# A forward transform over D in halves (even and odd columns) in place of quarters (remainders modulo 4), in a fused spectral-filter and GEGLU training step

## The chip, the cores and the metric

The kernel runs on one core of a Trainium2 chip. The core has five engines with a queue each: TensorE (PE in the profile; its weight loads are shown as PEld), VectorE (DVE), ScalarE (ACT), GpSimd (POOL) and SyncE (SP, which here only issues DMAs). The metric is the device time of one execution in microseconds, the median of several runs.

## The reference

Two branches of one layer are mixed by a gate, and the outputs are the layer's value and all gradients of it with respect to the inputs (except `B_x`, which is a constant that the kernel never reads: the FFN branch runs on `A_x`).

```python
x = A_x                                             # (1, 2048, 576), bf16
g = sigmoid((x * gate_w).sum(-1, keepdims=True))
a = irfft2(rfft2(x) * (A_w_r + 1j * A_w_i))         # over S=2048 and D=576; weights (2048, 289)
b = (gelu(x @ B_w_gate) * (x @ B_w_up)) @ B_w_down  # F = 4608
out = g * a + (1 - g) * b
# returned: out, and its vector-Jacobian product with grad_out for
# A_x, A_w_r, A_w_i, B_w_gate, B_w_up, B_w_down, gate_w
```

Both the forward transform of `x` and that of `g * grad_out` are needed: the first for `a` and for the gradient of the spectral weights, the second for the gradient of `x` through the filter and again for that of the weights. All transforms are done as matrix products with tables of sines and cosines.

## The kernel before

**Tiles.** S is split as 16 tiles `t` of 128 rows (row 16 p + t lies on partition p). `xn` and `dB` hold x and grad_out in this form, `xT` and `dOT` hold the transposes: five chunks of columns of D, four of 128 (selected by `eo(c)`) and the last 64 columns, 512 to 575, in the fifth. Because the chunks of `xT` and `dOT` are also the contraction of the FFN's products, the rows of `w_gate`, `w_up` and the transposed `w_down` are loaded in the same order (`load_w`).

**Phase 1** runs over 18 groups `g` of 256 columns of F and in each over four pairs `m` (four tiles of S each; 72 "pairs" in all, numbered `pr`). A pair computes `z` (grad_out times w_down, line 444 and 449) and `xy` (x times w_gate and w_up, line 453 and 460), evacuates them on ACT, forms the derivatives of GELU on DVE, and stores three results to DRAM scratch (`scr`). In the same pair TensorE computes weight gradients of the group before it (`W_units`, line 572, 590, 604). The order on every engine is the program's order, written out by hand; nothing is planned at run time.

**The transforms** ride along in phase 1 as a list `fft` of small units. From pair 6 on, `fft_next` places some four units in each pair between the weight-gradient jobs. First comes the forward transform (`fwd_units`): for each of 16 tiles of x and then of grad_out, `u1` multiplies by the D table (PSUM tile `yps`, evacuated by ACT to `Y`) and `u2` multiplies by the table of the 16-point rotations `R` (PSUM `vps`, evacuated by ACT to `ve`), combines parts on DVE into `Vt`, and stores `Vt` to DRAM. Then come the middle units (filter products) and the inverse. All units and `z` share one PSUM tile of two banks (tag `z`, `bufs=1`), so each must be evacuated before the next.

**The forward transform over D before.** A column d is 4 k + r. `eo(c)` takes every fourth column, so that chunk c of `xT` holds the columns with remainder c. For each remainder, only 73 frequencies need a product (`QF`); the other frequencies are sums and differences of the four remainders' results. `u1` makes four products with 2 x 73 = 146 columns, one for each remainder (line 633), and two with 4 x 73 = 292 columns for the last 64 columns of D (line 636). `u2` makes two products of 292 columns (line 651), and five DVE operations (lines 656 to 663) put the remainders together to 289 frequencies.

**Tables** are built at the start: `iotas` writes index columns on POOL, `build_D` forms angles on DVE or POOL and `sines` evaluates them on ACT. Before, there are three calls: the forward table `D4` (four columns of 73), the tail's `D4` (`D4t`, scaled on POOL by masks of the remainder, line 173), and `Dt` of 145 columns for the inverse, wholly on POOL up to its last step.

**The load of w_down.** For each next group the quarters of the load are issued on SP at the end of the pairs: in pair 0 the parts 0 (w_gate, w_up) and 1 (two transposing DMAs, into `wdT`'s fifth chunk and into `wtmp`), in pair 1 part 2 (a 32 KB copy within `wdT` and the store of `wtmp` to DRAM scratch `wscr`), in pair 2 part 3 (`wscr` back into `wdT` in the order of remainders). The first reader is `z` of the next group, after pair 3.

**Phase 2** (from about 950 us) reads `scr` back and makes the output and the gradient of x, line 1273.

Of the kernel before, what the change touches and what calls it, by code (L numbers as in the profile page):

```python
# [30 lines left out]
FG = 256  # L31
# [10 lines left out]
QF = 73  # L42
# [3 lines left out]
def eo(c):  # L46

    return slice(c, 512, 4)
# [16 lines left out]
def iotas(nc, res, unit):  # L65
    tb = Tables()
    G, V = nc.gpsimd, nc.vector
    kw = dict(allow_small_or_imprecise_dtypes=True)
    tb.halfpi = res.tile([P, 1], F32, name="halfpi")
    V.memset(tb.halfpi[:], math.pi / 2)  # L70
    tb.pi = res.tile([P, 1], F32, name="pi")
    V.memset(tb.pi[:], math.pi * EPS_SCALE)
    tb.warm = res.tile([P, 1], F32, name="warm")
    nc.scalar.activation(tb.warm[:], tb.halfpi[:], ACT.Sin)
    tb.lrow = unit([HF], F32, name="lrow")
    G.iota(tb.lrow[:], pattern=[[1, HF]], base=0, channel_multiplier=0, **kw)
    tb.dcol = res.tile([P, 8], F32, name="dcol")
    G.iota(tb.dcol[:, 0:4], pattern=[[1, 4]], base=0, channel_multiplier=4, **kw)
    for r in (LO, HI):
        G.iota(tb.dcol[r, 4:5], pattern=[[0, 1]], base=512, channel_multiplier=1, **kw)  # L80
    G.iota(tb.dcol[:, 5:7], pattern=[[1, 2]], base=0, channel_multiplier=2, **kw)
    G.iota(tb.dcol[:, 7:8], pattern=[[0, 1]], base=257, channel_multiplier=2, **kw)
    G.iota(tb.dcol[32:64, 7:8], pattern=[[0, 1]], base=256, channel_multiplier=2, **kw)
    tb.dn = res.tile([P, 8], F32, name="dn")
    V.tensor_scalar(tb.dn[:], tb.dcol[:], 1.0 / D, None, op0=ALU.mult)
    tb.late = []
    tb.Dt = []
    tb.Rt = []
    return tb


def iotas_R(nc, tb, res, unit):
# [15 lines left out]
    r4_i = res.tile([P, 1], I32, name="r4_i")  # L108
    tb.r4 = res.tile([P, 5], F32, name="r4_f")

    def parity():
        V.tensor_single_scalar(par_i[:], tb.qcol_i[:], 1, op=ALU.bitwise_and)
        V.tensor_copy(tb.par[:, 1:2], par_i[:])
        V.tensor_scalar(tb.par[:, 0:1], tb.par[:, 1:2], -1.0, 1.0, op0=ALU.mult, op1=ALU.add)
        V.tensor_scalar(tb.kadd[:, 0, 1:2], tb.par[:, 1:2], float(S // 2), float(S // 4), op0=ALU.mult, op1=ALU.add)
        V.tensor_single_scalar(r4_i[:], tb.qcol_i[:], 3, op=ALU.bitwise_and)
        V.tensor_copy(tb.r4[:, 4:5], r4_i[:])
        for r in range(4):
            G.tensor_scalar(tb.r4[:, r:r + 1], tb.r4[:, 4:5], float(r), None, op0=ALU.is_equal)
# [8 lines left out]
def build_D(nc, tb, unit, c0, n, w):  # L128

    V, G = nc.vector, nc.gpsimd  # L130
    step = 2.0 * math.pi / D
    TS = (G if c0 else V).tensor_scalar
    X = unit([n, w], F32, name="XD")
    y = unit([n, w], F32, name="yD")
    for c in range(n):
        TS(y[:, c, :], tb.lrow[:, 0:w], tb.dn[:, c0 + c:c0 + c + 1], MAGIC, op0=ALU.mult, op1=ALU.add)
    TS(y[:], y[:], -MAGIC, -float(D), op0=ALU.add, op1=ALU.mult)
    o = unit([n, 2, w], name="Dt")

    if c0 > 4:  # L140
        for c in range(n):
            G.tensor_scalar(X[:, c, :], tb.lrow[:, 0:w], tb.dcol[:, c0 + c:c0 + c + 1], None, op0=ALU.mult)
        G.tensor_tensor(X[:], X[:], y[:], op=ALU.add)

    def angles():
        for c in range(n if c0 <= 4 else 0):
            V.scalar_tensor_tensor(X[:, c, :], tb.lrow[:, 0:w], tb.dcol[:, c0 + c:c0 + c + 1], y[:, c, :],
                                   op0=ALU.mult, op1=ALU.add)
        V.scalar_tensor_tensor(y[:], X[:], -1.0, X[:], op0=ALU.mult, op1=ALU.max)

    def sines():
        if c0 == 0:
            v = o[:].rearrange("p (o r) c l -> p o (r c) l", o=2)
            co, si = v[:, :, 0:4:3, :], v[:, :, 1:3, :]
            yv, Xv = (t[:].rearrange("p (o r) l -> p o r l", o=2) for t in (y, X))
        else:
            co, si, yv, Xv = o[:, :, 0, :], o[:, :, 1, :], y[:], X[:]
        nc.scalar.activation(co, yv, ACT.Sin, bias=tb.halfpi[:], scale=-step)
        nc.scalar.activation(si, Xv, ACT.Sin, scale=-step * EPS_SCALE)
        if c0 == 0:  # L160
            tb.D4 = o
        elif c0 > 4:
            tb.Dt = [o[:, c] for c in range(n)]

    def tails():
        tl = tb.D4t = unit([2, 2, 4, w], name="Dt")
        G.memset(tl[HI, 0], 0.0)
        G.memset(tl[LO, 1], 0.0)
        for k, h in enumerate((LO, HI)):
            for r in range(4):  # L170
                for c in range(2):
                    b = 3 * c if r % 2 == 0 else 2 - c
                    G.tensor_scalar(tl[h, k, r // 2, b], o[h, 0, c], tb.r4[h, r:r + 1], None, op0=ALU.mult)
    return angles, sines, tails


# [99 lines left out]
def kernel(  # L276
# [24 lines left out]
    wscr = [dram.tile([512, FG], BF16, name=f"wscr{k}") for k in range(2)]  # L301
# [19 lines left out]
    def load_w(g, part, tails=LD):  # L321
# [4 lines left out]
        if part == 0:  # L326
            wgu = wts[g][0]
            for w, c0 in ((B_w_gate, 0), (B_w_up, FG)):
                cols = slice(c0, c0 + FG)
                LD.dma_start(wgu[:, 0:4, cols], w[0:512, fsl].rearrange("(p r) f -> p r f", r=4))  # L330
                for r in (LO, HI):
                    tails.dma_start(wgu[r, 4, cols], w[512:D, fsl])
# [4 lines left out]
        elif part == 2:  # L337
            wdT = wts[g][1]
            LD.dma_start(wdT[LO, 4, :], wdT[HI, 4, :])
            LD.dma_start(wscr[g % 2][:].rearrange("(c p) f -> p c f", p=P), wtmp[0][:])  # L340
        else:
            LD.dma_start(wts[g][1][:, 0:4, :], wscr[g % 2][:].rearrange("(p r) f -> p r f", r=4))
# [282 lines left out]
    def fwd_units(src, dst, scale, ps=pftile):  # L625
        ys = {}

        def u1(t):
            def f():
                yps = ps()  # L630
                for o in range(2):
                    for r, bs in ((2 * o, slice(0, 4, 3)), (2 * o + 1, slice(1, 3))):
                        nc.tensor.matmul(yps[:, o, 0:4 * QF].rearrange("p (b l) -> p b l", b=4)[:, bs, :], lhsT=src[:, r, t, :],  # L633
                                         rhs=tb.D4[:, r], start=(r % 2 == 0), stop=False)
                for o in range(2):
                    nc.tensor.matmul(yps[:, o, 0:4 * QF], lhsT=src[:, 4, t, :],
                                     rhs=tb.D4t[:, t % 2, o].rearrange("p b l -> p (b l)"), start=False, stop=True)
                ys[t] = unit([2, 4 * QF], name="Y")
                if scale is None:
                    nc.scalar.copy(ys[t][:], yps[:, :, 0:4 * QF])  # L640
                else:
                    nc.scalar.activation(ys[t][:], yps[:, :, 0:4 * QF], ACT.Copy, scale=scale[:, t:t + 1])
            return f

        def u2(t):
            def f():
# [3 lines left out]
                for o in range(2):  # L650
                    nc.tensor.matmul(vps[:, o, 0:4 * QF], lhsT=R, rhs=Y[:, o], start=True, stop=True)
                Vt = half([2, DF], name="Vt")
                ve = unit([8, QF], F32, name="ve")
                M = unit([2, 2, 2, QF], F32, name="vm")
                nc.scalar.copy(ve[:].rearrange("p (o b) l -> p o (b l)", o=2), vps[:, :, 0:4 * QF])
                V.tensor_tensor(M[:, 0].rearrange("p u v l -> p v u l"), ve[:, 0:4].rearrange("p (v u) l -> p v u l", u=2),
                                ve[:, 4:8].rearrange("p (v u) l -> p v u l", u=2), op=ALU.add)
                V.tensor_tensor(M[:, 1, 0], ve[:, 0:2], ve[:, 4:6], op=ALU.subtract)
                V.tensor_tensor(M[:, 1, 1], ve[:, 6:2:-3], ve[:, 2:8:5], op=ALU.subtract)
                up = Vt[:, :, 0:2 * (HF - 1)].rearrange("p c (k l) -> p k c l", k=2)[:, :, :, 0:QF]  # L660
                dn = Vt[:, :, DF - 1:0:-1].rearrange("p c (k l) -> p k c l", k=2)[:, :, :, 0:QF - 1]
                V.tensor_tensor(up, M[:, :, :, 0], M[:, :, :, 1], op=ALU.add)
                V.tensor_tensor(dn, M[:, :, :, 0, 0:QF - 1], M[:, :, :, 1, 0:QF - 1], op=ALU.subtract)
# [4 lines left out]
    def tail_table():  # L668
# [4 lines left out]
        for k, r in ((2, P), (3, 32)):  # L673
            o = 512 * (k - 2)
            for c in range(2):
                nc.tensor.transpose(tp_[:, c, o:o + r], tb.Dt[k - 1][0:r, c, 0:P], ident[0:r, 0:r])
            for c in range(2):
                nc.tensor.transpose(tp_[0:n, c, o + 256:o + 256 + r], tb.Dt[k - 1][0:r, c, P:HF], ident[0:r, 0:r])
# [5 lines left out]
        for c in range(2):  # L684
            for e, sb in enumerate((tb.Dt[2][32:64], ot)):
# [263 lines left out]
    D0 = build_D(nc, tb, unit, 0, 4, QF)  # L949
# [4 lines left out]
    D4 = build_D(nc, tb, unit, 4, 1, QF)  # L954
    D2 = build_D(nc, tb, unit, 5, 3, HF)
# [6 lines left out]
    D2[0]()  # L962
# [83 lines left out]
    for g in range(NG):  # L1046
# [3 lines left out]
        for m in range(NPR):  # L1050
# [122 lines left out]
            if m < 3 and g + 1 < NG:  # L1173
                for part in ((0, 1), (2,), (3,))[m]:
                    load_w(g + 1, part)
# [247 lines left out]
```

## Time and profile before

| | |
|---|---|
| median of 3 runs | 1384.02 us (1384.02 to 1384.03) |
| profiled execution | 1384.02 us, span 1382.2 us |
| PE busy | 1363.2 us (99%), 10186 matmuls |
| DVE, ACT, POOL busy | 783.2, 701.6, 259.8 us |
| stretch 0 to 60 us (tables, first group) | PE busy 56.47 |
| stretch 60 to 300 us (forward transform inside it) | PE busy 235.28, DVE 185.10, ACT 180.46 |
| stretch 300 to 950 us (filter and inverse inside it) | PE busy 642.86 |
| stretch 950 to 1382 us (phase 2) | PE busy 428.62 |

Matmuls are pipelined: the profile gives each a duration that reaches to the modelled end of its result, so durations of neighbours overlap, and "busy" is the time in which at least one is under way. What a product costs in a stream is the distance from its start to the start of the next one. In rows of groups, the columns are line, engine, operation, tile written and tiles read, shape, count, then busy time and mean duration, then the idle time of the engine just before and what ended it. A row of the timeline is start, length, engine, line, operation and count; rows of one operation that follow each other are merged.

### The profile page before, as it was taken

Reading aid. Unit: us, or ns where it says so; the run is one execution under the profiler, and the core shown is the slowest. Engines: PE = TensorE matmul, PEld = TensorE weight load, DVE = VectorE, ACT = ScalarE, POOL = GpSimd, SP = SyncE. Lnnn points to the kernel's source line nnn. Section 1 sums busy time; section 2 is a strip of 40 time slices with the busy share of each in tenths; the row PEclk is TensorE's granted clock in tenths of the full one; section 3 lists DMA queues with packets and bytes.
Section 4 is the critical chain, followed back from the end, with each engine's and each line's share of the span. In section 5 each row is a group of like instructions: output and inputs, shape, how many; then the busy total and the mean of one; then the engine's idle time right before and its main releaser. Section 6 shows DMA issues by size and latency. Waiting matters only on the chain.

```text
span 1382.2 us, 25988 instructions
## 1 busy us (share of the span) xinstructions
PE 1363.2 (99%) x10186; PEld 908.5 (66%) x10272; DVE 783.2 (57%) x1514; ACT 701.6 (51%) x1300; POOL 259.8 (19%) x513
## 2 busy tenths in 40 slices
PE   9999999999999999999999999999999999999998
PEld 6556656566556556556656566556777777777776
DVE  7887777865988877885676766550001642122101
ACT  7877777768877877866766767651000000000000
POOL 7001110132445444331110111110000110000000
PEclk9999999999999999999999999999999999999999
DMA  7434444466466665555556556659999997787773
GB/s 234 126 88 136 128 131 119 120 169 158 129 162 159 161 160 150 143 156 151 135 157 154 159 158 166 168 128 274 196 190 197 235 193 164 158 161 168 155 150 88
DMA packets 512423, 218.95 MB, mean 158 GB/s; under 512 B 312010, under 2 KB 503180, under 8 KB 512300
## 3 DMA queue, kind: packets, MB, share of 16 engines
q1 hardware_dynamic: 495178, 191.89, 59.3%
q0 software_dynamic: 14912, 24.24, 6.1%
q8 instruction: 80, 1.31, 0.4%
q10 hardware_dynamic: 2210, 1.15, 0.4%
q14 instruction: 43, 0.35, 0.1%
HBM read 45.51 MB, written 98.30 MB: 104 GB/s over the span
## 4 chain that ended last, share of the span: by engine, by line
PE 92%; ACT 3%; DVE 2%; DMA 1%; issue 1%; ACTq 0%; SPq 0%; DVEq 0%
PE acc L1273 31%; PE wps L590 16%; PE xy L460 16%; PE wps L572 10%; PE z L444 8%; PE wps L604 2%; PE xy L453 2%; PE z L449 2%; DMA wgu<-in_B_w_up_dram 1%; DMA xn<-in_A_x_dram 1%; PE pf L914 1%; PE pf L840 1%; PE pf L751 1%; PE pf L633 1%; PE pf L916 1%
## 5 line engine op out<-in xcount | busy, mean ns | idle before, releaser
L1273 PEld LDWEIGHTS <-pin 128*128 128x128 bf16 x3456 | 337.5, 98 | 86.3 <-issue 0.3
L590 PE MATMUL wps<-dH,xn 128*128 128x512 bf16 x1135 | 270.0, 379 | 0.9
L460 PE MATMUL xy<-wgu,xT 128*128 128x512 bf16 x1083 | 258.6, 380 | 8.2 <-issue 6.8
L460 PEld LDWEIGHTS <-xT 128*128 128x128 bf16 x1152 | 106.4, 98 | 132.9 <-issue 24.8
L590 PEld LDWEIGHTS <-xn 128*128 128x128 bf16 x1152 | 111.4, 98 | 118.4 <-issue 0.6
L1290 ACT COPY bo<-acc 128x288 f32<-128x288 f32 x32 | 12.8, 399 | 305.0 <-PE acc L1273 271.6
L572 PE MATMUL wps<-dB,A 128*128 128x288 bf16 x1152 | 153.3, 286 | 0.1
L597 POOL DMA_DIRECT2D out_dram<-dw x134 | 72.8, 547 | 421.9 <-ACT dw L541 380.4
L1273 PE MATMUL acc<-wgT,pin 128*128 128x288 bf16 x1152 | 143.8, 286 | 0.0
L1273 PE MATMUL acc<-wuT,pin 128*128 128x288 bf16 x1152 | 143.6, 286 | 0.0
L1273 PE MATMUL acc<-wd_all,pin 128*128 128x288 bf16 x1152 | 142.6, 286 | 0.0
L444 PE MATMUL z<-wdT,dOT 128*128 128x256 bf16 x1152 | 137.7, 273 | 0.0
L572 PEld LDWEIGHTS <-A 128*128 128x128 bf16 x1152 | 112.0, 98 | 33.0 <-issue 0.3
L472 ACT ACTIVATE da<-z,omg 128x256 bf16<-128x256 f32 x288 | 112.0, 471 | 31.9 <-PE z L449 31.8
L444 PEld LDWEIGHTS <-dOT 128*128 128x128 bf16 x1152 | 112.3, 98 | 21.6 <-issue 0.6
L1345 DVE SCALAR_TENSOR_TENSOR f32t<-gwf,dlog,b16t 128x576 f32<-128x576 f32 x16 | 13.1, 818 | 171.8 <-DMA b16t<-dxa_scr 171.8
L481 ACT CAST xb<-xy 128x512 bf16<-128x512 f32 x144 | 85.0, 590 | 48.2 <-PE xy L460 48.2
L479 ACT ACTIVATE q<-xy 128x512 bf16<-128x512 f32 x144 | 87.8, 613 | 17.0 <-PE xy L460 13.5
L482 ACT CAST hu<-xy 128x512 bf16<-128x512 f32 x144 | 87.4, 607 | 0.0
L518 DVE TENSOR_TENSOR xb<-xb,sg 128x1024 bf16<-128x1024 bf16 x48 | 33.1, 690 | 85.8 <-ACT sg L510 85.7
L541 ACT CAST dw<-wps 128x512 bf16<-128x512 f32 x72 | 42.3, 590 | 54.8 <-PE wps L590 52.4
L1304 DVE SCALAR_TENSOR_TENSOR b16t<-b16t,g,f32t 128x576 bf16<-128x576 bf16 x16 | 13.1, 818 | 98.1 <-DMA b16t<-a_scr 97.9
(239 smaller groups left out, 1700.3 us busy)
## 6 DMA issues: line engine op xcount, KB each, us to landing
scr<-dH SPq DMA_DIRECT2D x144, 256.0 KB, 3.4
scr<-A SPq DMA_DIRECT2D x72, 256.0 KB, 2.5
out_dram<-dw POOLq DMA_DIRECT2D x134, 64.0 KB, 2.5
wd_all<-in_B_w_down_dram SPq DMA_DIRECT2D x3, 1728.0 KB
out_dram<-dwd POOLq DMA_DIRECT2D x34, 144.0 KB, 2.9
scr_p<-Vt SPq DMA_DIRECT2D x32, 145.0 KB, 2.8
wgu<-in_B_w_gate_dram SPq DMA_DIRECT2D x18, 256.0 KB, 4.1
wgu<-in_B_w_up_dram SPq DMA_DIRECT2D x18, 256.0 KB, 3.4
```

Of the source, the lines that this page charges most:

```text
L444: nc.tensor.matmul(zo(t), lhsT=dOT[:, ci, t, :], rhs=wdT[:, ci, :], start=(t % 4 < 2 and ci == 0), stop=False)
L460: nc.tensor.matmul(xy[k][:, t % 2, :], lhsT=xT[:, ci, t, :], rhs=wgu[:, ci, :], start=False, stop=(ci == 3))
L472: nc.scalar.activation(da[:, t, :], z[:, t % 2, t // 2, :], ACT.Copy, scale=omg32[:, 4 * m + t:4 * m + t + 1])
L479: nc.scalar.activation(q[:, h, :], xy[:, :, 0:FG], ACT.Square)
L481: nc.scalar.copy(xb[:, h, :], xy[:, :, 0:FG])
L482: nc.scalar.copy(hu[:, h, :], xy[:, :, FG:2 * FG])
L518: V.tensor_tensor(xb[:], xb[:], s[:], op=ALU.mult)
L541: wcopy[0](out, in_)
L572: nc.tensor.matmul(wps[:, :288], lhsT=tl(0, t)[:, fch * P:(fch + 1) * P], rhs=dB[:, t, h * 288:(h + 1) * 288], start=(t == 0), stop=(t == ...
L590: nc.tensor.matmul(wps[:].rearrange("p a b -> p (a b)"), lhsT=xn[:, t, c * P:(c + 1) * P], rhs=kt[t // 4][1][:, t % 4].rearrange("p k f -> ...
L597: wst[0].dma_start(ov[:, c, fsl], dw[:, k, :])
L1273: nc.tensor.matmul(acc[:, :288], lhsT=src[:, r, :], rhs=w_of(r)[:, h * 288:(h + 1) * 288], start=(first and r == 0), stop=(last and r == F ...
```

## The change

The forward transform goes over the two parities of d instead of the four remainders. `eo(c)` now takes 128 columns of one parity (c = 0, 1 the even ones, 2, 3 the odd ones, below 512). The table of the forward transform is that of 145 columns (`HF`) for each chunk, the same that the inverse uses, so the separate quarter table is gone. `u1` makes four products of 290 columns and two of 290 for the tail; `u2` two of 290, and two DVE operations in place of five. The tail's table is scaled on DVE by the two parity masks instead of on POOL by four remainder masks. `build_D` is called for two, two and one columns of 145. In `load_w`, `wdT` gets its rows from `wtmp` by four copies within SBUF, without the DRAM scratch, and the parts 0, 1 and 2 are issued at the ends of pairs 0, 1 and 2. The rows of w_gate and w_up are loaded in the new order by as many DMAs as before.

```diff
 def eo(c):
-    return slice(c, 512, 4)
+    return slice(256 * (c % 2) + c // 2, 256 * (c % 2) + 256, 2)
...
-    G.iota(tb.dcol[:, 0:4], pattern=[[1, 4]], base=0, channel_multiplier=4, **kw)
+    for par in range(2):
+        G.iota(tb.dcol[:, 2 * par:2 * par + 2], pattern=[[256, 2]], base=par, channel_multiplier=2, **kw)
...
-        for r in range(4):
-            G.tensor_scalar(tb.r4[:, r:r + 1], tb.r4[:, 4:5], float(r), None, op0=ALU.is_equal)
...
     def tails():
-        for k, h in enumerate((LO, HI)):
-            for r in range(4):
-                for c in range(2):
-                    b = 3 * c if r % 2 == 0 else 2 - c
-                    G.tensor_scalar(tl[h, k, r // 2, b], o[h, 0, c], tb.r4[h, r:r + 1], None, op0=ALU.mult)
+        for k, r in enumerate((LO, HI)):
+            for par in range(2):
+                V.tensor_scalar(tl[r, k, par], o[r, 0], tb.par[r, par:par + 1], None, op0=ALU.mult)
...
     def load_w(g, part, tails=LD):
-                LD.dma_start(wgu[:, 0:4, cols], w[0:512, fsl].rearrange("(p r) f -> p r f", r=4))
+                LD.dma_start(wgu[:, 0:4, cols].rearrange("p (e k) f -> p e k f", e=2),
+                             w[0:512, fsl].rearrange("(k p e) f -> p e k f", e=2, p=P))
...
-        elif part == 2:
+        else:
             wdT = wts[g][1]
             LD.dma_start(wdT[LO, 4, :], wdT[HI, 4, :])
-            LD.dma_start(wscr[g % 2][:].rearrange("(c p) f -> p c f", p=P), wtmp[0][:])
-        else:
-            LD.dma_start(wts[g][1][:, 0:4, :], wscr[g % 2][:].rearrange("(p r) f -> p r f", r=4))
+            for par in range(2):
+                for h, r in enumerate((LO, HI)):
+                    LD.dma_start(wdT[r, 2 * par:2 * par + 2, :], wtmp[0][par:P:2, h:4:2, :])
...
         def u1(t):
-                for o in range(2):
-                    for r, bs in ((2 * o, slice(0, 4, 3)), (2 * o + 1, slice(1, 3))):
-                        nc.tensor.matmul(yps[:, o, 0:4 * QF].rearrange("p (b l) -> p b l", b=4)[:, bs, :], lhsT=src[:, r, t, :],
-                                         rhs=tb.D4[:, r], start=(r % 2 == 0), stop=False)
-                for o in range(2):
-                    nc.tensor.matmul(yps[:, o, 0:4 * QF], lhsT=src[:, 4, t, :],
-                                     rhs=tb.D4t[:, t % 2, o].rearrange("p b l -> p (b l)"), start=False, stop=True)
+                for par, j in [(par, j) for par in range(2) for j in range(2)] + [(0, 2), (1, 2)]:
+                    ci, tab = (4, 4 + 2 * (t % 2) + par) if j == 2 else (2 * par + j, 2 * par + j)
+                    nc.tensor.matmul(yps[:, par, :2 * HF], lhsT=src[:, ci, t, :], rhs=tb.Dt[tab].rearrange("p c l -> p (c l)"),
+                                     start=(j == 0), stop=(j == 2))
...
         def u2(t):
-                M = unit([2, 2, 2, QF], F32, name="vm")
-                V.tensor_tensor(M[:, 0]..., ve[:, 0:4]..., ve[:, 4:8]..., op=ALU.add)
-                V.tensor_tensor(M[:, 1, 0], ve[:, 0:2], ve[:, 4:6], op=ALU.subtract)
-                V.tensor_tensor(M[:, 1, 1], ve[:, 6:2:-3], ve[:, 2:8:5], op=ALU.subtract)
-                V.tensor_tensor(up, M[:, :, :, 0], M[:, :, :, 1], op=ALU.add)
-                V.tensor_tensor(dn, M[:, :, :, 0, 0:QF - 1], M[:, :, :, 1, 0:QF - 1], op=ALU.subtract)
+                V.tensor_tensor(Vt[:, :, 0:HF], v[0], v[1], op=ALU.add)
+                V.tensor_tensor(Vt[:, :, DF - 1:HF - 1:-1], v[0][:, :, 0:HF - 1], v[1][:, :, 0:HF - 1], op=ALU.subtract)
...
-    D0 = build_D(nc, tb, unit, 0, 4, QF)
+    D0 = build_D(nc, tb, unit, 0, 2)
     D0[0]()
...
-    D4 = build_D(nc, tb, unit, 4, 1, QF)
-    D2 = build_D(nc, tb, unit, 5, 3, HF)
+    D2 = build_D(nc, tb, unit, 2, 2)
+    D2[0]()
+    D4 = build_D(nc, tb, unit, 4, 1)
...
-    D2[0]()
...
             if m < 3 and g + 1 < NG:
-                for part in ((0, 1), (2,), (3,))[m]:
-                    load_w(g + 1, part)
+                load_w(g + 1, m)
```

## The prediction

> **What bounds the kernel now.** I read the page first: the busy shares and the chain that ended last.
>
> ```profile
> PE 1363.2 (99%) x10186; PEld 908.5 (66%) x10272; DVE 783.2 (57%) x1514; ACT 701.6 (51%) x1300; POOL 259.8 (19%) x513
> PE 92%; ACT 3%; DVE 2%; DMA 1%; issue 1%; ACTq 0%; SPq 0%; DVEq 0%
> ```
>
> TensorE (PE) is busy for 99% of the span and is 92% of the chain; 1382.2 less 1363.2 leaves 19.0 us in which it stood idle anywhere. But a share is a mean over stages, and the change sits in one of them, the forward transform. Line 633, the first product of the transform, runs from 75 to 280 us by the view of that line, so next comes the table by stretches around it. Columns: length, then busy time of PE, its weight loads, DVE, ACT and POOL, the granted TensorE clock, and the DMA share.
>
> ```profile
> 60.00:100.00 40.00, 37.64 (x271) 23.11 (x274) 33.91 (x72) 32.75 (x63) 5.69 (x10) 1.00 0.43 119
> 100.00:150.00 50.00, 49.35 (x362) 30.82 (x365) 38.90 (x83) 36.68 (x67) 6.47 (x12) 1.00 0.44 124
> 150.00:200.00 50.00, 49.53 (x352) 30.30 (x356) 38.38 (x80) 37.02 (x70) 5.40 (x10) 1.00 0.46 130
> 200.00:250.00 50.00, 49.42 (x359) 30.58 (x363) 37.91 (x80) 36.45 (x66) 5.39 (x10) 1.00 0.45 126
> 250.00:300.00 50.00, 49.34 (x359) 30.55 (x363) 36.00 (x76) 37.55 (x69) 8.57 (x16) 1.00 0.46 130
> ```
>
> PE idles 2.36 + 0.65 + 0.47 + 0.58 + 0.66 = 4.7 us of these 240. DVE is busy for 185.1 of the 240 (77%): well loaded, but it has 55 us to spare, and the clock is at full rate throughout. Whom PE waits for here is in the view of waits of PE over 60 to 300 us (total, times, longest):
>
> ```profile
> PE xy L460 <- issue: 1.6, 10, 0.2
> PE pf L651 <- ACT Y L640: 1.1, 1, 1.1
> PE pf L633 <- ACT ve L655: 1.0, 2, 0.7
> ```
>
> No wait of PE on DVE is there at all. The two that name an engine are on ACT. So in this stage matmul columns are what time is made of.
>
> **The products of u1 (line 633 and 636), by the timeline of PE:**
>
> ```profile
> 207.28 0.41 PE L651 MATMUL pf<-Y,Rt 128*128 128x292 bf16 x2
> 207.54 1.02 PE L460 MATMUL xy<-wgu,xT 128*128 128x512 bf16 x4
> 208.40 1.89 PE L590 MATMUL wps<-dH,xn 128*128 128x512 bf16 x8
> 210.13 0.43 PE L633 MATMUL pf<-Dt,dOT 128*128 128x146 bf16 x4
> 210.39 0.41 PE L636 MATMUL pf<-Dt,dOT 128*128 128x292 bf16 x2
> 210.64 1.02 PE L590 MATMUL wps<-dH,xn 128*128 128x512 bf16 x4
> ...
> 212.75 1.15 PE L572 MATMUL wps<-dB,A 128*128 128x288 bf16 x8
> ```
>
> Only starts are used, since the ends are modelled and overlap. Today u1 is four products of 146 columns in 210.39 - 210.13 = 0.26 us (65 ns each) and two of 292 in 210.64 - 210.39 = 0.25 us: 0.51 us. The changed u1 is six products of 290 columns with the same six stationary tiles. The nearest row is L572: eight products of 288 columns from 212.75 to 213.73, where the next group starts, so 122.5 ns each. With two columns more I take 124 ns: 6 x 124 = 0.74 us. The difference is 0.23 us, and u1 runs 32 times (16 tiles of x, 16 of grad_out): **+7.3 us on PE**. Bounds: at 122 ns a product it is 0.22 x 32 = +7.0; at the 130 ns that a pair of L651 takes (207.28 to 207.54) it is (0.78 - 0.51) x 32 = +8.6. Nothing hides it, because PE has nothing else to stand behind.
>
> The Trainium skill, "TensorE: Matmul & The Clock Gate", section "Back-to-back issue gap", sets the gap at N/2.4 + 2.5 ns, and says besides that a stream in which every matmul loads its own weights holds about 81 ns at N=128. By that second figure four narrow products would cost at least 0.32 us today, u1 0.57 us, and the change only about +5.4 us (estimate from that page). The row above has 65 ns each with a weight load apiece, so here the row decides.
>
> **u2, PE side.** Two products of 292 columns become two of 290; at 0.42 ns a column, (379 - 286)/(512 - 288) by the mean durations of L590 and L572, that is 128 columns in all, 0.05 us. Nothing.
>
> **u2, DVE side.** Today's five operations, from the groups by form (busy, mean ns, idle before):
>
> ```profile
> L656 DVE TENSOR_TENSOR vm<-ve 128x292 f32<-128x292 f32 x32 | 14.7, 461 | 20.0 <-ACT ve L655 19.6
> L658 DVE TENSOR_TENSOR vm<-ve 128x146 f32<-128x146 f32 x32 | 9.7, 304 | 0.0
> L659 DVE TENSOR_TENSOR vm<-ve 128x146 f32<-128x146 f32 x32 | 9.7, 303 | 0.0
> L662 DVE TENSOR_TENSOR Vt<-vm 128x292 bf16<-128x292 f32 x32 | 14.8, 464 | 1.1
> L663 DVE TENSOR_TENSOR Vt<-vm 128x288 bf16<-128x288 f32 x32 | 14.7, 459 | 1.1
> ```
>
> They sum to 1.99 us. The changed u2 has two, of 290 and 288 columns; the same shape (the inverse's yo, line 925 and 926) takes 493 and 479 ns, so 0.97 us. DVE loses 1.02 x 32 = 33 us of work between 75 and 293 us. On the path this is worth what PE waits for DVE there, which is 0 by the waits. The bound on the gain is every named engine wait of PE in the stretch, 1.1 + 1.0, and 0.2 for the turn of R: -2.3 us. I take 0, for the releasers are ACT, and ACT's copies hardly shrink (584 to 580 columns). The unit of scratch that u2 no longer takes frees ring space; PE waits for none of it.
>
> **The load of wdT (load_w).** The third quarter of each group no longer writes wtmp to DRAM and reads it back, it copies it within SBUF: one DMA of 32 KB as before, and four of 64 KB. Per group SP issues 6 at the end of pair 0, 2 transposes at the end of pair 1 and 5 at the end of pair 2, against 8, 2 and 1 today. What has to be met is the first z of the next group. Group 5 is the tightest I found:
>
> ```profile
> 248.73 0.68 SPq L342 DMA_DIRECT2D wdT<-wscr  x1
> ...
> 256.95 1.26 PE L444 MATMUL z<-wdT,dOT 128*128 128x256 bf16 x10
> ```
>
> 8.2 us lie between issue and use (9.0 for the group at 411 us, 9.3 at 720 us). Five issues at 0.68 us put the last at 248.73 + 2.7 = 251.4. A copy inside SBUF of today lands by this row:
>
> ```profile
> wdT<-wdT SPq DMA_DIRECT2D x17, 32.0 KB, 3.3
> ```
>
> 251.4 + 3.3 = 254.7, so 2.2 us ahead of z: cost 0. Behind the five on SP stands the store of Vt, issued at 255.45 today when DVE has written it; SP is free from 249.4, so the queue is clear again at 252.1. The transposes move one pair later, to the end of pair 1 (230.16 here), land in 3.7 us by the median of wtmp in the view of DMAs and are first read 15 us later. If each copy held SP as long as a transpose does (1.3 us), the last would be issued at 248.73 + 0.68 + 3 x 1.3 = 253.3 and, landing in 5.8 us as the loads of Vp from scr_g do by the same view, arrive at 259.1: 2.2 us late here, 1.4 and 1.1 at the two next. So 0 to +4.7 us; I take 0, by the nearest row, which is the copy to the same tile.
>
> The Trainium skill, "DMA: Bandwidth & Descriptors", section "Anatomy of one DMA — SWDGE (gpsimd) path", gives about 2.0 us fixed per DMA (for another path than SP's), which speaks against splitting. If that were paid one after another, four copies would add 8 us and z of group 5 would wait (estimate). But the six wgu loads of a group issue within 3.9 us and land together here, so the fixed part overlaps.
>
> **Start.** Tables are wider (145 columns for 73), but fewer, and 16 scalings on POOL (9.9 us from 13.93) become four on DVE. DVE begins its tables when dn is there, at 2.7 us, and reaches the copy of the w_down tile at 5.94. Changed: two products with the column (0.25 each), one scaling (0.45), two STT (0.4), one of 290 (0.56) for the first half, and 0.4 x 2 + 0.56 for the second, which now stands ahead of that copy: about 6.3, so the copies come up to 0.4 us later; two index fills fewer (0.15 each) take that back. The tail table's four on DVE, at most 0.36 each by the 128x576 scaling of dB, start at 11.6 and end by 13.0, under the 1.28 us that DVE waits there until 13.12; were that cover gone, 1.4 us. First used at 75 us. I take 0. The gain is bounded by the waits of PE for DVE before 60 us, 0.8 for a copy of dOT and 0.3 at the gate: -1.1; the loss by the 0.4 above.
>
> **Sum.** Profiled execution: 1384.02 us, span 1382.2, so 1.8 us outside it; the median of the three runs is the same 1384.02. +7.3 + 0 + 0 + 0 + 0 gives **1391.3 us**.
>
> **Rivals.**
> 1. *The added columns fall partly into standing waits.* The 2.3 us of ACT waits lie where ACT is late (the sines of R near 80 to 91 us); longer u1 gives ACT time. With the bound of the start, +7.3 - 2.3 - 1.1 = +3.9: 1387.9. Against it: waits elsewhere in the stretch are nearly nil. Chance 0.12.
> 2. *wdT becomes the wait.* z stands first in each group, so all of PE stands. Price +4.7 from the three tightest: 1396; if SP also is blocked behind a store at the end of pair 2 in most of 17 groups, 1 us each, +17: 1408. It begins when issue to landing exceeds 8.2 us. For it: SP is often held for DVE (107 us for Vt in total). Against it: the estimate of 6.0 us. Chance 0.09.
> 3. *Not slower: DVE paced the stage after all.* The relief of 33 us would reach PE through u2: ve and Vt freed sooner, and the one PSUM tile that z and the units share handed over sooner. It decides from 0.23 us of hidden PE wait per tile and would, at a third of the relief, give -11 + 7.3: 1380. Against it: eight L590 fill 208.40 to 210.13 at 216 ns each, the rate of the four L460 before them (207.54 to 208.40), so no gap is hidden where L633 takes over. Chance 0.06.
>
> **How the numbers follow.** My forecast (wide products at their rate, nothing else moves) gets 0.73, from +6 to +8.6. The range reaches below to rival 1 and above into the smaller part of rival 2: 1387.9 to 1395.0. About 0.2% (2.8 us) is what a measurement can tell from no change. Slower by more: forecast, rivals 1 and 2, less what rival 1 may exceed: 0.93. Within: 0.04, faster 0.03, both of rival 3.
>
> **What would show it.** Right: u1 six products in 0.74 us; PE idle of 60 to 300 us again near 5 us while DVE's busy time there falls by some 33 us; z of group g+1 waiting for no wdT copy; the time before phase 2 longer by 7 us and phase 2 (line 1273) unchanged. Wrong: a pitch of 290 columns below 115 ns; a wait of L444 for a DMA into wdT; the first z after 8.5 us; PE idle in the stage falling by more than 2.5 us.

## The result and the profile after

The changed kernel takes 1389.87 us (median of 6 runs, 1389.5 to 1390.37) against 1384.03 us before in the same session. The ratio is 1.0039, with a 95% interval from 1.0026 to 1.0052, so the change costs 5.8 us. The forecast was 1391.3 us in a range from 1387.9 to 1395.0, slower.

The page of the changed kernel, the busy shares and the chain that ended last:

```profile
PE 1370.5 (99%) x10186; PEld 913.3 (66%) x10272; DVE 752.4 (54%) x1418; ACT 702.8 (51%) x1300; POOL 245.4 (18%) x486
PE 95%; ACT 2%; DVE 2%; issue 1%; POOL 0%; ACTq 0%; DVEq 0%; POOLq 0%
```

It has as many matmuls as before, 7.3 us more of busy TensorE, 30.8 us less of busy DVE, and a longer span. The stretches around the forward transform (columns as before: length, then PE, its weight loads, DVE, ACT, POOL, clock, DMA share, GB/s):

```profile
100.00:150.00 50.00, 49.36 (x346) 30.81 (x348) 28.89 (x55) 35.20 (x65) 5.79 (x11) 1.00 0.39 113
200.00:250.00 50.00, 49.58 (x345) 30.74 (x348) 28.44 (x53) 35.75 (x63) 6.46 (x12) 1.00 0.40 109
```

DVE has fallen from 38.90 and 37.91 to 28.89 and 28.44 us of each 50. TensorE is as full as it was, and it gets through fewer matmuls in the same time (346 and 345 against 362 and 359), because those of u1 are wider. The timeline of PE shows one u1:

```profile
211.60 1.89 PE L570 MATMUL wps<-dH,xn 128*128 128x512 bf16 x8
213.33 0.91 PE L613 MATMUL pf<-Dt,dOT 128*128 128x290 bf16 x6
214.08 1.02 PE L570 MATMUL wps<-dH,xn 128*128 128x512 bf16 x4
```

Six products of 290 columns fill 213.33 to 214.08, 0.75 us, where four of 146 and two of 292 took 0.51.

To see where the 5.65 us between the two spans (1387.9 and 1382.2, by the trace 1387.89 and 1382.24) arose, I take the same five events in both traces: the first product of z in group 0, in group 1, in pair 6 (where the transforms begin to be placed), in pair 23 (the forward transform is done) and in the last pair. The rows of the kernel before come first, then those of the changed one:

```profile
7.73 0.38 PE L444 MATMUL z<-wdT,dOT 128*128 128x256 bf16 x2
43.80 0.27 PE L444 MATMUL z<-wdT,dOT 128*128 128x256 bf16 x1
67.38 0.38 PE L444 MATMUL z<-wdT,dOT 128*128 128x256 bf16 x2
298.92 0.38 PE L444 MATMUL z<-wdT,dOT 128*128 128x256 bf16 x2
915.68 0.38 PE L444 MATMUL z<-wdT,dOT 128*128 128x256 bf16 x2
```

```profile
7.53 0.39 PE L424 MATMUL z<-wdT,dOT 128*128 128x256 bf16 x2
42.67 0.38 PE L424 MATMUL z<-wdT,dOT 128*128 128x256 bf16 x2
66.20 0.38 PE L424 MATMUL z<-wdT,dOT 128*128 128x256 bf16 x2
304.74 0.38 PE L424 MATMUL z<-wdT,dOT 128*128 128x256 bf16 x2
921.44 0.38 PE L424 MATMUL z<-wdT,dOT 128*128 128x256 bf16 x2
```

| stretch | before, us | after, us | difference |
|---|---|---|---|
| to the first z | 7.73 | 7.53 | -0.20 |
| to group 1 | 36.07 | 35.14 | -0.93 |
| to pair 6 | 23.58 | 23.53 | -0.05 |
| forward transform | 231.54 | 238.54 | **+7.00** |
| filter and inverse | 616.76 | 616.70 | -0.06 |
| to the end | 466.56 | 466.45 | -0.11 |

So the forward transform costs 7.0 us more, within 0.3 us of the forecast's 7.3, and the first 44 us give 1.1 us back, which the forecast had set to nothing. The row to the first z says little: in the twelve traces of this case, of both kernels and of the experiments, that instant lies anywhere between 7.32 and 8.43 us. The row to group 1 repeats: the changed kernel and the four experiments on it that do not hold up its start have 35.01 to 35.14 us there.

Most of the gain to group 1 is seen at one place, 0.67 of the 0.93 us. The timelines of DVE and of POOL before, then of both after:

```profile
29.09 1.12 DVE L523 TENSOR_SCALAR xb<-s 128x1024 bf16<-128x1024 bf16 x1
29.05 0.87 POOL L243 IOTA k2B<- 128x128 f32 x1
```

```profile
28.66 0.43 DVE L503 TENSOR_SCALAR xb<-s 128x1024 bf16<-128x1024 bf16 x1
25.04 0.88 POOL L223 IOTA k2B<- 128x128 f32 x1
```

The same scaling of 128x1024 took 1.12 us before, beside an index fill of POOL (IOTA) that began 0.04 us earlier. It took 0.43 us after, when POOL had begun that fill at 25.04. DVE was that much later with its copy of dOT, and TensorE waited for this copy 0.8 us before and 0.2 us after, by the waits of PE over the first 60 us, before and after:

```profile
PE pf L399 <- DVE dOT L406: 0.8, 1, 0.8
```

```profile
PE pf L379 <- DVE dOT L386: 0.2, 1, 0.2
```

The other 0.25 us lie at the gate's products: from the first of them to the next z it takes 1.01 us before, with a wait of 0.28 for DVE, and 0.76 us after, without. DVE had begun its last copies of xT there at 9.82 before and at 9.41 after. What brought them forward was not tested on its own.

POOL came to its fills earlier. Before, the 16 scalings of the tail table stood ahead of them and kept POOL until 23.85 us. After, they are gone and POOL's other tables are done sooner, so that it stands idle for 12.80 us and goes on at 20.58, when DVE's values are there. That was read from the traces; the second set of experiments asks whether the fill beside the scaling is the cause.

### The profile page after: what moved, and what is told of

Same layout as the page of the kernel before. It is cut to its first block, busy times and chain, and to the rows that moved or that the text cites. A ratio compares the mean times of both kernels' runs of the same rounds, so it can differ in the third digit from the quotient of the medians.

```text
span 1387.9 us, 25926 instructions
## 1 busy us (share of the span) xinstructions
PE 1370.5 (99%) x10186; PEld 913.3 (66%) x10272; DVE 752.4 (54%) x1418; ACT 702.8 (51%) x1300; POOL 245.4 (18%) x486
## 4 chain that ended last, share of the span: by engine, by line
PE 95%; ACT 2%; DVE 2%; issue 1%; POOL 0%; ACTq 0%; DVEq 0%; POOLq 0%
PE acc L1245 31%; PE xy L440 17%; PE wps L570 17%; PE wps L552 10%; PE z L424 9%; PE wps L584 2%; PE xy L433 2%; PE pf L613 2%; PE z L429 2%; PE pf L887 1%; PE pf L813 1%; PE pf L630 1%; PE pf L724 1%; PE pf L889 1%; PE pf L860 1%
```

## The experiments

The theory: the forward transform pays for its columns on TensorE, DVE's relief and the new load of wdT are worth nothing, and the start gains about 1 us. The rivals: DVE paces the stage in part, or the load of wdT carries part of the result.

**A dose of narrow products, in the kernel before.**

```diff
                 yps = ps()
+                for r in range(4):
+                    nc.tensor.matmul(yps[:, r // 2, 292:438].rearrange("p (b l) -> p b l", b=2), lhsT=src[:, r, t, :],
+                                     rhs=tb.D4[:, r], start=True, stop=True)
                 for o in range(2):
```

> The kernel before, with four more products of 146 columns in each u1, into columns 292 to 437 of the same PSUM tile that nothing reads; the results stay as they were. Theory (TensorE columns set the time of the forward transform): four at 65 ns, 32 times, +8.4 us, so 1392.4. Rival (DVE paces the stage and TensorE has room): no change, 1384.0 within 1 us.

Measured: 1391.89 us against 1384.2 in the same session, ratio 1.0047 (1.0034 to 1.0059): +7.7. One u1 in its timeline of PE:

```profile
215.11 0.42 PE L632 MATMUL pf<-Dt,dOT 128*128 128x146 bf16 x4
215.38 0.42 PE L636 MATMUL pf<-Dt,dOT 128*128 128x146 bf16 x4
215.64 0.41 PE L639 MATMUL pf<-Dt,dOT 128*128 128x292 bf16 x2
```

The added four take 0.27 us (215.11 to 215.38) and come through almost whole: TensorE has no room in this stage, and the rival, that DVE paces it and TensorE has room, falls.

**DVE's work put back, in the changed kernel.**

```diff
                 v = [ve[:, 0], ve[:, 1]]
+                M = unit([8, 73], F32, name="vm")
+                vf = ve[:].rearrange("p o c l -> p (o c l)")
+                Mf = M[:].rearrange("p b l -> p (b l)")
+                V.tensor_tensor(Mf[:, 0:292], vf[:, 0:292], vf[:, 288:580], op=ALU.add)
+                V.tensor_tensor(Mf[:, 292:438], vf[:, 0:146], vf[:, 290:436], op=ALU.subtract)
+                V.tensor_tensor(Mf[:, 438:584], vf[:, 146:292], vf[:, 434:580], op=ALU.subtract)
```

> The changed kernel, with three DVE operations added to each u2 that take the 292, 146 and 146 columns of the kernel before into a tile that nothing reads: 32 times 1.07 us, 34 us of DVE work. Theory: TensorE does not wait for DVE there, so 1389.9 within 0.5 us. Rival (the relief of DVE paid for the part by which the measured +5.8 us stays under the +7.3 us of the columns): 1391.3 or more.

Measured: 1389.85 us, against 1389.87 for the changed kernel without it. The view of waits of PE over 60 to 300 us of this run:

```profile
PE pf L613 <- ACT ve L633: 1.0, 2, 0.7
PE pf L630 <- ACT Y L618: 0.8, 1, 0.8
```

These are the changed kernel's own two waits, with 25.0 us more of busy DVE in that stretch (176.38 against 151.37; neighbours overlap, so this is less than the 34 us of their durations). By the starts of z the forward transform takes 238.53 us, against 238.54 without this work. So three quarters of the 33.7 us of which the change relieved DVE here (185.10 to 151.37) were worth nothing; that the last quarter was worth nothing too is argued from the waits, for in neither kernel does TensorE wait for DVE in this stretch.

**The DRAM trip of wdT put back, in the changed kernel.**

```diff
-        else:
+        elif part == 2:
             wdT = wts[g][1]
             LD.dma_start(wdT[LO, 4, :], wdT[HI, 4, :])
-            for par in range(2):
-                for h, r in enumerate((LO, HI)):
-                    LD.dma_start(wdT[r, 2 * par:2 * par + 2, :], wtmp[0][par:P:2, h:4:2, :])
+            LD.dma_start(wscr[g % 2][:].rearrange("(c p) f -> p c f", p=P), wtmp[0][:])
+        else:
+            LD.dma_start(wts[g][1][:, 0:4, :].rearrange("p (e k) f -> p e k f", e=2),
+                         wscr[g % 2][:].rearrange("(k p e) f -> p e k f", e=2, p=P))
...
-                load_w(g + 1, m)
+                for part in ((0, 1), (2,), (3,))[m]:
+                    load_w(g + 1, part)
```

> The changed kernel, with the load of wdT as before: wtmp to DRAM and back, in the four parts of the old order. Theory: hidden in both forms, 1389.9 within 0.5 us. Rival (the shorter path without DRAM traffic is what gave 1.5 us back): 1391.3. Second rival (the five copies at the end of pair 2 are late for z): 1389 or less.

Measured: 1389.66 us, against 1389.87 without the trip. The interval of the ratio (1.0023 to 1.0046) shuts out the first rival's 1391.3 but not the second's 1389. The traces shut out that too: from group 1 to the last pair every stretch agrees with the changed kernel's within 0.02 us, and neither run's waits of PE, over the whole span, name a load of wdT. Both forms of the load are hidden.

**Half of the main products left out, in the changed kernel.**

```diff
-                for par, j in [(par, j) for par in range(2) for j in range(2)] + [(0, 2), (1, 2)]:
+                for par, j in [(0, 2), (1, 2)] + [(par, j) for par in range(2) for j in range(2)]:
                     ci, tab = (4, 4 + 2 * (t % 2) + par) if j == 2 else (2 * par + j, 2 * par + j)
-                    nc.tensor.matmul(yps[:, par, :2 * HF], lhsT=src[:, ci, t, :], rhs=tb.Dt[tab].rearrange("p c l -> p (c l)"),
-                                     start=(j == 0), stop=(j == 2))
+                    n = 2 * HF if j == 2 else 146
+                    nc.tensor.matmul(yps[:, par, :n], lhsT=src[:, ci, t, :], rhs=tb.Dt[tab].rearrange("p c l -> p (c l)")[:, 0:n],
+                                     start=(j == 2), stop=(j == 1))
```

> The changed kernel, with the four main products of u1 cut to their first 146 columns (the other half of the transform is left out, so the output is not the reference's; the tail's two products stay whole and come first). Theory: the whole loss is the columns, 4 x (126 - 66) ns x 32 = 7.7 us less, 1382.2, which is below the kernel before because the start got faster by 1.2 us. Rival (part of the loss is elsewhere in the change): 1384 or more.

Measured: 1382.51 us against 1384.2 before, ratio 0.9983 (0.9974 to 0.9992), and 7.4 us under the changed kernel. With the columns of u1 back at about the width of before (four of 146 and two of 290), all of the loss is gone, the forward transform takes 231.10 us against 231.54 before, and the kernel is below its predecessor by 1.7 us. In its timeline of PE the six products run from 213.04 to 213.54, 0.50 us:

```profile
213.04 0.67 PE L614 MATMUL pf<-Dt,dOT 128*128 128x290 bf16 x6
213.54 0.65 PE L552 MATMUL wps<-dB,A 128*128 128x288 bf16 x4
```

**The start: two orders of the tail table, in the kernel before.** The first issues the 16 scalings behind the index fills; the second has DVE scale the table.

```diff
         parity()
-        D4[2]()
...
                 elif m == 1:
                     next(makeB)
+                    D4[2]()
```

> The kernel before, with the 16 scalings of the tail table on POOL issued after the index fills of the table B (in pair 1 instead of pair 0). Theory (the start of the changed kernel is faster because POOL's index fills no longer run beside a DVE scaling at 29 us, which took 1.12 us in place of 0.43): that DVE operation is short again, TensorE's wait of 0.83 us at 34.84 goes, 1383.0 to 1383.4. Rival (the start gained from fewer and differently ordered table operations on DVE): 1384.0.

```diff
             for r in range(4):
-                for c in range(2):
-                    b = 3 * c if r % 2 == 0 else 2 - c
-                    G.tensor_scalar(tl[h, k, r // 2, b], o[h, 0, c], tb.r4[h, r:r + 1], None, op0=ALU.mult)
+                bs = slice(0, 4, 3) if r % 2 == 0 else slice(2, 0, -1)
+                V.tensor_scalar(tl[h, k, r // 2, bs], o[h, 0], tb.r4[h, r:r + 1], None, op0=ALU.mult)
```

> The kernel before, with the tail table scaled on DVE in 8 operations of 146 columns instead of 16 on POOL. Theory: as the last one, -0.8 us from the wait at 34.84, less up to 0.7 us if the 8 operations (2 us) outlast DVE's pause of 1.28 us at 12 us: 1383.2 to 1383.9. Rival: 1384.0 or more.

Measured: 1384.57 us (1383.11 to 1386.24) and 1383.77 us (1383.72 to 1384.79), against 1384.31 in the same session; ratios 0.9996 (0.9987 to 1.0005) and 0.9993 (0.9984 to 1.0002). The times can't tell either from no change, and the first missed its forecast of 1383.0 to 1383.4. The trace of the first can tell the mechanism. In its timelines of DVE and POOL the fill of k2B is at 25.80 and the DVE scaling is short again; in its waits of PE the wait is down to 0.2 us.

```profile
29.44 0.43 DVE L523 TENSOR_SCALAR xb<-s 128x1024 bf16<-128x1024 bf16 x1
25.80 0.87 POOL L243 IOTA k2B<- 128x128 f32 x1
```

```profile
PE pf L399 <- DVE dOT L406: 0.2, 1, 0.2
```

From the first z (8.13) to that of group 1 (43.52) it takes 35.39 us, against 36.07 before: 0.68 us of the changed kernel's 0.93 by the order on POOL alone. In the second the eight DVE operations outlast DVE's pause and cost more than was allowed for: the same stretch takes 36.56 us. Its time lies in the forecast range all the same, which is luck as far as the trace tells: its profiled execution is 0.3 us shorter than that of the kernel before because it gains 0.5 us from the last pair on, where nothing was changed.

**Sixteen scalings put back on POOL, in the changed kernel**, into a tile that nothing reads.

```diff
+        idle = unit([16, 73], name="idle")
+        for k, r in enumerate((LO, HI)):
+            for b in range(8):
+                nc.gpsimd.tensor_scalar(idle[r, 8 * k + b], o[r, 0, 0, 0:73], tb.par[r, 0:1], None, op0=ALU.mult)
```

> The changed kernel, with 16 scalings of 64x73 on POOL (9.9 us in the kernel before) put back after the tail table, into a tile that nothing reads, so that POOL reaches the index fills as late as before. Theory: a DVE scaling is stretched by one of the fills again and TensorE waits 0.7 to 0.8 us more, 1390.6 to 1390.8. Rival: 1389.9.

Measured: 1389.93 us, no change where 1390.6 to 1390.8 was expected. It could not test whether a fill holds up a scaling: the scalings ran from 11.16 for 9.09 us, POOL was done at 20.25 and began its next work at 20.44, when DVE's values were there, and the fill of k2B came at 24.89 (25.04 without them). It shows that the 16 scalings alone do not make POOL late. In the kernel before they do, because there POOL begins them 2.8 us later, at 13.93, and ends at 23.85. The next two experiments put work right ahead of the fills.

**Eight more index fills, and eleven scalings instead, in the changed kernel.**

```diff
+    spin = unit([2, 2, 16, 2], F32, name="spin")
+    for _ in range(8):
+        G.iota(spin[:], pattern=[[0, 4], [2, 16], [0, 2]], base=0, channel_multiplier=0, **kw)
     G.iota(k2[:], pattern=[[0, 4], [2, 16], [0, 2]], base=0, channel_multiplier=0, **kw)
```

> The changed kernel, with eight more index fills of 128x128 on POOL (0.87 us each, 7 us) ahead of those of the table B, into a tile that nothing reads; they run from about 25 to 32 us. The run with 16 scalings put back did not test the theory, because POOL was done with them before it could begin the fills. Theory (an index fill on POOL holds up a DVE scaling that runs beside it): two to three of the DVE scalings between 28 and 33 us take 0.8 to 1.2 us in place of 0.43, TensorE's wait at 33.7 grows from 0.16 by 0.8 to 1.9 us, 1390.7 to 1391.8. Rival (the long DVE scaling before was chance, or came from something else): all stay at 0.43, 1389.9.

```diff
+    spin = unit([3, HF], F32, name="spin")
+    G.memset(spin[:], 0.0)
+    for _ in range(11):
+        G.tensor_scalar(spin[:], spin[:], 0.5, 1.0, op0=ALU.mult, op1=ALU.add)
     G.iota(k2[:], pattern=[[0, 4], [2, 16], [0, 2]], base=0, channel_multiplier=0, **kw)
```

> As the last, with eleven scalings of 128x435 fp32 on POOL (some 7 us by the 626 ns of such a one before) in place of the eight index fills. Theory (it is the index fill that holds DVE): DVE's scalings stay at 0.43 and the time at 1389.9. Rival (any work on POOL does it): as the run with the fills, 1390.7 to 1391.8.

Measured: 1390.81 us with the fills (ratio to before 1.0043, 1.0029 to 1.0057), +0.9 over the changed kernel; 1394.01 us with the scalings (1.0066, 1.0051 to 1.0082), +4.1. The first interval covers the changed kernel's 1.0039, so there the trace has to decide: to group 1 it takes 36.30 us, against 35.14 without the fills. The timelines of DVE and POOL and the waits of PE of the run with the fills:

```profile
31.32 0.62 DVE L470 TENSOR_SCALAR s<-q 128x1024 bf16<-128x1024 bf16 x1
32.65 1.04 DVE L472 TENSOR_SCALAR q<-q 128x1024 bf16<-128x1024 bf16 x1
32.54 0.86 POOL L226 IOTA k2B<- 128x128 f32 x1
```

```profile
PE pf L382 <- DVE dOT L389: 1.0, 1, 1.0
```

Two of DVE's three scalings in that stretch take 0.62 and 1.04 us in place of 0.42, its operations on two tensors keep their 0.69, and TensorE's wait is back, at 1.0 us. So an index fill can hold up a DVE scaling, and that wait is on the path. It does not always: the third scaling ran among the fills too and took its 0.43 us. Its row and those of two fills:

```profile
28.79 0.43 DVE L506 TENSOR_SCALAR xb<-s 128x1024 bf16<-128x1024 bf16 x1
28.00 0.86 POOL L225 IOTA spin<- 128x128 f32 x1
30.79 0.86 POOL L225 IOTA spin<- 128x128 f32 x1
```

In these four cases what counts is the fill that is already running when the scaling begins. The three long scalings end 0.28 us after the end of that fill: at 30.21 after 29.93 in the kernel before, here at 31.93 after 31.65 and at 33.69 after 33.41. The short one began at 28.79, only 0.06 us before its fill ended (28.86), and the next fill, begun at 28.93, did not hold it. The run with POOL's scalings:

```profile
27.73 1.04 DVE L501 TENSOR_TENSOR A<-xb,hu 128x1024 bf16<-128x1024 bf16 x1
34.93 0.78 DVE L473 TENSOR_SCALAR q<-q 128x1024 bf16<-128x1024 bf16 x1
25.73 9.71 POOL L226 TENSOR_SCALAR spin<-spin 128x435 f32<-128x435 f32 x11
```

Here the theory falls in its narrow form, that it is the index fill. Scalings on POOL of 128x435 hold DVE as well, and its operations on two tensors too (1.04 in place of 0.69). POOL's own mostly take 0.88 us, against 0.57 for the first of them and 0.63 for the one in the kernel before. The cost is beyond the rival's 1390.7 to 1391.8 too. In the profiled execution (1392.31 us) TensorE's wait is 2.2 us and it takes 37.87 us to group 1, 2.7 more than without the scalings; the other three executions are 1.5 to 1.9 us longer still, which is not traced:

```profile
PE pf L389 <- DVE dOT L390: 2.2, 1, 2.2
```

**A version of the kernel before with the masks and the tail table behind the fills.**

```diff
-        parity()
-        D4[2]()
+        parity[0]()
...
                     next(makeB)
+                    parity[1]()
+                    D4[2]()
```

> The kernel before, with the 16 scalings of the tail table and the masks of the remainder that they use (two operations on DVE, four on POOL) issued behind the index fills, in pair 1. Theory: 0.7 us from the DVE scaling that is no longer held, and up to 0.3 us from DVE's two operations at 11.5 us: 1383.0 to 1383.3, the fastest of all. Rival: 1384.0.

Measured: 1383.49 us (1383.39 to 1385.28) against 1384.29 (1384.04 to 1386.26) in the same session, ratio 0.9995 (0.9986 to 1.0004). It has the lowest median of all the kernels that compute the whole, 0.8 us under the one before, but the interval includes 1, which is no change. In its trace the first z to that of group 1 takes 43.02 - 8.01 = 35.01 us, as in the changed kernel, and TensorE waits for DVE neither at the copy of dOT nor at the gate. So by the trace the order of the setup work alone gives the kernel before the changed kernel's start; the times can't confirm it.

## Why the prediction was right, point by point

**What bounds the kernel: right.** No wait of TensorE on DVE in the stage, so DVE's 33 us should be worth nothing. Putting such work back, 25 us of busy time, gave 1389.85 us against 1389.87. TensorE's idle time of 60 to 300 us is 4.0 us, 4.7 before, as the prediction's signs had it. The four added products of 146 columns took 0.27 us, 68 ns each with a weight load apiece. The Trainium skill, "TensorE: Matmul & The Clock Gate", section "Back-to-back issue gap", has about 81 ns for such a stream at 128 columns, which does not describe this one.

**The price of u1: right, a little low.** Forecast 0.74 us for the six products and 0.51 for the six of before. Over all 32 the median is 748 and 514 ns, so 234 ns and 7.5 us instead of 7.3. The stage grew by 7.0. Of the difference 0.1 is u2, whose narrower products were put at 0.05 and called nothing. The other 0.4 is what the first rival foresaw in kind, so that "nothing hides it" was a little too strong: the wait of u2's product for Y, behind the sines of R, went from 1.07 to 0.83 us; the remaining 0.2 I have not traced. The run with added narrow products is alike, 8.4 us of products and a stage longer by 7.95 (306.90 - 67.41 by the starts of z, against 231.54). That the columns are the whole loss is shown by the run that left half of the main products' columns out.

**DVE's side: right in kind.** The two operations take 460 and 452 ns where 493 and 479 were assumed.

**The load of wdT: right.** The copies land 2.3 us after issue (3.3 was assumed), by this row of the DMAs of the changed kernel, and SP is free 3.3 us before the next store (255.74 and 259.05 in group 5):

```profile
wdT<-wtmp SPq DMA_DIRECT2D x68, 64.0 KB, 2.3
```

and for group 5, in the timelines of SP and PE:

```profile
253.08 2.66 SPq L322 DMA_DIRECT2D wdT<-wtmp  x4
261.85 1.36 PE L424 MATMUL z<-wdT,dOT 128*128 128x256 bf16 x11
```

Issue of the last ends at 255.74, and z is at 261.85. The upper end, 4.7 us, was not needed.

**The start: the one term that was mis-sized.** It was set to 0 between -1.1 and +0.4, and measured -1.13 up to group 1, at the end of its bounds. The 0.20 before the first z are within the scatter of that instant; the 0.93 behind it are the two waits that the bound was made of, 0.67 at the copy of dOT and 0.25 at the gate. The steps on DVE were right or a little dear: the copies of the w_down tile began at 5.81 and not at 6.3, the four scalings of the tail took 1.02 us from 11.25 and were hidden. What failed is that the work taken from POOL was given no effect: nothing in the prediction follows what POOL does next once its 9.9 us of scalings are gone, and TensorE's wait for DVE's copy of dOT was listed as a bound, not followed to its cause, though the timeline has a DVE scaling of 1.12 us in a row of scalings of 0.42.

**The sum.** +7.0 for the stage, -1.13 up to group 1 and -0.22 for the three other stretches (-0.05, -0.06 and -0.11) make the 5.65 us of the spans. Rival 2 (wdT) and rival 3 (DVE) are refuted by the runs above. Of the 2.3 us that rival 1 puts into the stage's waits 0.4 came, and the start reached its bound; these two, for the most part, brought the time 1.4 us under the forecast, inside a range whose lower end was set for just that. The mechanism on which the forecast rests, columns on a TensorE that waits for nobody, is the one measured.

## What to carry to other kernels

Where TensorE is full and waits for nobody, price a change by the distance from start to start of its products, and ignore what it takes off the other engines: here the further split saved 7 us of columns for 33 us of DVE time that nobody waited for. In the first microseconds, where DVE is on the path, look at POOL beside it, and follow a known wait back to an operation that takes longer than others of its form; in this kernel the order of the setup work on POOL decided which DVE operation met a fill.

## What the runs showed of the hardware that was not expected

An index fill on POOL (128x128 fp32, 0.87 us) that had 0.34 to 0.84 us left when a DVE scaling of 128x1024 bf16 began stretched it from 0.42 to 0.62, 1.04 and 1.12 us, so that it ended 0.28 us after the fill. A fill that began after the scaling did not stretch it (0.43), and two-tensor operations beside the fills stayed at 0.69. POOL scalings of 128x435 fp32 stretched both, up to 0.78 from 0.43 and up to 1.04 from 0.69. POOL scalings of 64x73 bf16 hardly touched either: the kernel before ran DVE's scalings of 128x1024 at 0.43 and 0.42 beside them (20.75 and 21.89 us), and its two-tensor operations at 0.69 and 0.73. POOL's own took longer instead: the 16 scalings took 13.44 us where the first experiment on the start put them beside DVE's large operations, against 9.92 before.

The Trainium skill, "GPSIMD Engine Reference", section "1. Specifications", says that POOL shares its SBUF interfaces with VectorE and contends with DVE instructions in a two-port mode or with two SBUF inputs. Two-tensor operations with both inputs in SBUF are the second kind; that the scalings are the first, no run here shows. With that, the runs agree for both kinds where POOL scales 128x435, and only for the scalings where it fills an index table.
